# Loads, weights and a new hand-written order in a fused linear-attention and MLP kernel

## The chip, the cores and the metric

The kernel runs on one core of one Trainium2 chip. The metric is the device time of one execution in microseconds (us), lower is better; the profile's span runs from the first to the last instruction of the same program.

## The reference

Two pre-norm blocks in a row on 2048 tokens of width 512, all in bf16. Layer norm here has no weights. Block A is linear attention with 32 heads of 16 columns, block B a two-layer perceptron with 1792 hidden columns.

```python
def _A_ref(x, wqkv, wo):                       # H = 32, Dh = 16
    qkv = (lambda x, *d: x.transpose(*d))((x @ wqkv).reshape(B, S, 3, H, Dh), 2, 0, 3, 1, 4)
    q, k, v = qkv[0], qkv[1], qkv[2]
    phi = lambda t: jnp.where(t > 0, t + 1, jnp.exp(t)) + 1e-6
    pq, pk = phi(q), phi(k)
    kv = jnp.einsum("bhsd,bhse->bhde", pk, v)
    z = jnp.einsum("bhsd->bhd", pk)
    num = jnp.einsum("bhqd,bhde->bhqe", pq, kv)
    den = jnp.einsum("bhqd,bhd->bhq", pq, z)[..., None] + 1e-6
    o = num / den
    return (lambda x, *d: x.transpose(*d))(o, 0, 2, 1, 3).reshape(B, S, D) @ wo

h = x + _A_ref(_layernorm(x, axis=-1), A_wqkv, A_wo)
h2 = h + _B_ref(_layernorm(h, axis=-1), B_w1, B_w2)      # relu(ln(h) @ w1) @ w2
```

## The kernel before

The 2048 tokens are 16 tiles of 128 rows (t = 0 to 15) in 4 chunks of 512 (c = 0 to 3); the 512 columns are 4 blocks of 128, the 1792 hidden columns 14. There is no loop over tiles in the code. A string, ORDER (lines 18 to 55), lists 568 words; each word is the name of a small function with its numbers (`K.7.3` is `op_K(7, 3)`), and the last lines walk the string and issue the instructions. So the order of the words of one engine is the order in which that engine executes; words of different engines stand in for each other only through the semaphores that the data need. The last number of a word on TensorE is mostly the PSUM bank (of 8) that it writes.

The words by engine, in the order of the stages:

- **SP**, the only engine that issues DMAs, all of them into one queue: `lx.t.n` loads n tiles of x from tile t; `lk`, `lq`, `lv`, `lo`, `l1`, `l2` load the weights for keys, queries, values, output, w1 and w2 (first block of 128 rows, number of blocks); `X.t` and `x.t` are transposing DMAs (lines 290 and 291) that write one tile of the normed x, or of the normed h, transposed into lnT; `wb.c` (line 450) writes the reciprocal denominators of chunk c to DRAM, eight `rb.c.h` (line 453) read them back, broadcast, into one buffer rr; `fd.t` stores a tile of the result. The weights l2 come in two halves of 7 blocks, `l2.0.7` and `l2.7.7`.
- **TensorE**: `warm` (matmuls of zeros at the start), `T` and `t` (transposes of a tile), `K.t` (keys of one tile, line 298, 4 matmuls of 512 columns), `Q.c.j` (queries, line 306), `G.t` (the state of keys against the normed x, line 350, into banks 4 to 7), `z`, `d4.c` (denominators of a chunk, line 422), `kv`, `m` (m = kv times wo), `h.t` (attention output, line 475), `p.c.f` and `ph` (first layer, line 490 and in halves 499), `f.t.b.f0.n` (second layer, line 519, 14 matmuls in two halves of 7).
- **ScalarE (ACT)**: `R` and `r` (reciprocal standard deviation, two steps), `E` (a transposed tile from PSUM to lnT), `F` and `U` (exp and relu of the keys), `qF` and `qU` (of the queries), `dl4` and `dx4` (logarithm and exp that make the reciprocal denominators), `gA`, `mA` (copies of G and m), `pA` (relu of the first layer), `nA` (the centred h, line 257).
- **VectorE (DVE)**: `S` and `A`, `s` and `a` (mean and variance), `N` and `n` (normed x, centred h), `M` and `D`, `qM` and `qD` (min and sum that finish the feature maps), `za` to `zh` (sum of the keys), `gD`, `mD` (copies), `kx`, `dm.c.jb.2` (line 466: queries times rr into pqs), `hD` (line 481: h), `pD` (relu of the first layer, line 510), `fo` (result).

Around the change the chain of one chunk is: `d4.c` on TensorE, `dl4.c` and `dx4.c` on ScalarE, `wb.c` and eight `rb.c` on SP, two `dm.c` on VectorE, then four `h` on TensorE, of which each reads all four blocks of pqs. rr has one buffer, so `rb` of a chunk waits for `dm` of the chunk before. pqs has eight blocks, two chunks. All loads of weights are free of waits for data. The words of SP before, from the start to the second chunk's `rb`:

```
lx.0.1 lx.1.1 lx.2.2 lk.0.2 lk.2.2 lx.4.2 lx.6.2 lq.0.4 lx.8.4 lx.12.4 X.5 X.6 X.7 lv.2.2 lv.0.2
X.8 X.9 X.13 X.12 X.11 X.10 X.14 X.15 lo.0.2 lo.2.2 l1.0.2 l1.2.2 wb.0 rb.0 (8) l2.0.7 wb.1 x.1 x.0 rb.1 (8) l2.7.7
```

Of the kernel before, what the change touches and what calls it, by code (L numbers as in the profile page):

```python
# [15 lines left out]


ORDER = """
table const masks warm.70.7.64 warm.2.7 lx.0.1 S.0 lx.1.1 S.1 A.0 R.0.1 A.1 lx.2.2 S.2 N.0.0.2 A.2 N.0.2.2 R.1.1
R.2.1 N.1 T.0.4.0.2 E.0.0.2 T.0.3.2.2 lk.0.2 S.3 lk.2.2 T.1.7 lx.4.2 N.2 A.3 E.0.2.2 E.1 lx.6.2 R.3.1 lq.0.4 S.4  # L20
N.3 K.0.0.0.2 K.0.0.2.2 T.2.5 E.2 S.5 A.4 K.1.6.0.2 S.6 F.0.1 K.1.6.2.2 T.3.1 E.3 K.2.3.0.2 K.2.3.2.2 U.1.1 A.5
lx.8.4 R.4.2 S.7 M.0.1 U.0.1 A.7 A.6 N.4 R.6.2 N.5 D.0.1 S.9 K.3.2.0.2 K.3.2.2.2 Q.0.3.1 F.1.1 T.4.0 F.3.1 M.1.1
Q.0.1.5 N.6 M.3.1 A.9 N.7 D.1.1 E.4 Q.0.0.4 lx.12.4 K.4.6 F.2.1 M.2.1 U.2.1 U.3.1 S.13 D.3.1 X.5 S.8 qF.0.0.2
A.13 K.5.7 Q.0.2.0 X.6 K.6.2 qU.0.0.2 F.4.2 U.4.2 S.11 X.7 lv.2.2 A.8 S.12 D.2.1 A.12 M.4.2 S.10 R.8.2 R.12.2
lv.0.2 K.7.3 qM.0.0.2 G.2 U.6.2 G.3 G.1 G.0 N.8 A.11 A.10 N.9 X.8 X.9 N.13 D.4.2 S.14 S.15 R.10.2 F.6.2 A.14
qU.0.2.2 X.13 N.12 A.15 N.11 qD.0.0.2 M.6.2 N.10 G.4 X.12 R.14.2 K.8.2 G.5 qF.0.2.2 D.6.2 qM.0.2.2 N.14 za.4.1
N.15 K.9.3 F.8.2 G.7 K.13.1 U.8.2 K.12.0 M.8.2 X.11 za.6.0 X.10 G.6 U.12.2 X.14 K.11.3 X.15 D.8.2 F.12.2
qD.0.2.2 K.10.2 F.10.2 U.10.2 K.14.0 za.8.0 M.12.2 zf M.10.2 lo.0.2 K.15.1 F.14.2 G.9 G.8 U.14.2 zhi D.10.2
D.12.2 M.14.2 zlo G.10 Q.1.1.3 D.14.2 z.2.1 lo.2.2 l1.0.2 z.0.1 z.1.1 z.3.1 zc G.14 zh d4.0.0 G.11 G.13 G.12
dl4.0 G.15 gD.0.2 Q.1.0.2 dx4.0 Q.1.2.0 l1.2.2 gA.2.2 kv.2.7 kv.0.7 kv.1.7 kv.3.7 qF.1.0.2 qU.1.0.2 qM.1.0.2  # L30
Q.1.3.1 Q.2.1.5 kx qD.1.0.2 m.0.2 m.3.7 m.2.6 m.1.3 qF.1.2.2 qU.1.2.2 qM.1.2.2 mD.2.2 Q.2.0.4 wb.0 Q.2.2.0
rb.0.0 Q.2.3.1 mA.0.2 rb.0.1 rb.0.6 rb.0.7 rb.0.4 rb.0.2 rb.0.3 rb.0.5 qF.2.0.2 dm.0.0.2 dm.0.2.2 h.1.2 qU.2.0.2
qD.1.2.2 hD.1 d4.1.5 s.1 a.1 qU.2.2.2 h.0.4 hD.0 l2.0.7 h.3.7 n.1 dl4.1 dx4.1 s.0 qF.2.2.2 a.0 n.0 h.2.2 hD.2
wb.1 hD.3 Q.3.1.5 Q.3.0.4 s.2 x.1 Q.3.2.6 x.0 s.3 Q.3.3.7 a.2 rb.1.2 rb.1.1 a.3 n.2 qF.3.0.2 qU.3.0.2 n.3
ph.0.0.2.0 t.2.5 t.3.4 qM.2.0.2 rb.1.0 rb.1.5 rb.1.7 rb.1.6 qM.2.2.2 r.0.4 qF.3.2.2 ph.0.2.0.0 ph.0.1.3.0 v.2
v.3 qM.3.0.2 ph.0.3.1.0 ph.0.1.3.1 qM.3.2.2 qD.2.2.2 rb.1.3 rb.1.4 qD.2.0.2 qU.3.2.2 l2.7.7 ph.0.0.2.1 qD.3.0.2
qD.3.2.2 ph.0.2.0.1 pA.0.0.2 ph.0.3.1.1 p.0.10.6 d4.2.2.2 dm.1.0.2 dm.1.2.2 dl4.2 dl4.3 dx4.2 wb.2 pD.0.2.2
dx4.3 rb.2.0 p.0.11.7 pD.0.10.2 h.4.2 hD.4 h.6.3 h.7.5 hD.6 rb.2.6 hD.7 s.4 h.5.6 rb.2.3 p.0.6.0 rb.2.2 s.6 a.4
hD.5 s.7 a.6 s.5 p.0.7.1 a.7 n.4 p.0.5.7 p.0.4.6 pA.0.6.2 rb.2.5 rb.2.7 rb.2.1 a.5 p.0.12.5 n.7 pD.0.4.2 n.6
p.0.9.4 rb.2.4 p.0.8.3 wb.3 x.7 x.4 n.5 dm.2.2.2 x.6 dm.2.0.2 p.0.13.6 f.0.1.0.7 h.9.2 pD.0.8.2 pD.0.12.2 hD.9  # L40
r.4.4 h.8.3 h.11.0 s.9 hD.8 h.10.2 x.5 rb.3.4 rb.3.3 rb.3.2 rb.3.7 rb.3.6 hD.11 p.1.1.5 hD.10 a.9 p.1.0.4 s.8
p.1.9.3 s.10 s.11 rb.3.1 p.1.8.2 a.10 a.8 a.11 pA.1.0.2 n.8 rb.3.0 r.8.4 n.10 n.9 f.0.1.7.7 f.1.7.0.7 pA.1.8.2
rb.3.5 dm.3.2.2 n.11 dm.3.0.2 fo.0 h.15.6 hD.15 x.11 h.14.5 s.15 hD.14 h.12.3 p.1.12.0 h.13.4 a.15 p.1.13.1
hD.12 s.14 s.12 hD.13 a.12 pA.1.12.2 f.1.7.7.7 a.14 s.13 a.13 r.12.4 n.13 fo.1 n.12 n.15 n.14 p.1.5.2 p.1.4.1
pD.1.4.2 x.9 x.10 x.8 p.1.2.5 p.1.3.6 pD.1.2.2 p.1.10.0 p.1.11.1 p.1.6.5 x.13 p.1.7.6 pA.1.10.2 pA.1.6.2 p.2.4.2
p.2.5.3 f.3.7.0.7 f.2.5.0.7 f.3.7.7.7 f.2.5.7.7 pA.2.4.2 x.15 fo.3 p.2.12.2 p.2.13.3 p.2.1.1 p.2.0.0 pA.2.12.2
pA.2.0.2 p.2.8.3 p.2.9.4 p.2.6.1 p.2.7.2 fo.2 fd.3 pD.2.6.2 pA.2.8.2 p.2.3.4 p.2.2.3 f.4.5.0.7 x.14 fd.2 fd.0
x.12 pA.2.2.2 f.4.5.7.7 fo.4 f.5.0.0.7 f.5.0.7.7 fd.1 p.3.2.5 p.3.3.6 fo.5 f.7.7.0.7 f.6.1.0.7 f.6.1.7.7 fo.6
p.3.7.3 p.3.6.2 f.7.7.7.7 fo.7 pA.3.2.2 pA.3.6.2 p.3.0.6 p.3.10.4 p.3.1.7 pA.3.0.2 p.3.11.5 p.3.9.3 pD.3.10.2
p.3.4.0 p.3.5.1 pA.3.4.2 p.3.8.2 fd.7 p.3.12.6 p.3.13.7 pD.3.8.2 p.2.11.3 pD.3.12.2 f.15.0.0.14.0.2 p.2.10.2  # L50
f.8.5.0.7 fo.15.0.2 pD.2.10.2 f.8.5.7.7 fd.5 f.13.4.0.7 fd.6 fd.4 f.13.4.7.7 fo.8 fd.8 fd.15.0.2 f.9.3.0.7 fo.13
fd.13 f.9.3.7.7 f.14.0.0.7 fo.9 f.14.0.7.7 fo.14 f.11.7.0.7 f.11.7.7.7 fo.11 f.10.6.0.7 fd.14 f.10.6.7.7 fo.10
fd.9 fd.10 f.12.2.0.7 f.12.2.7.7 fo.12 fd.11 fd.12 f.15.0.0.14.3.1 fo.15.3.1 fd.15.3.1 f.15.1.0.14.2.1 fo.15.2.1
fd.15.2.1
"""


# [512 lines left out]
```

## Time and profile before

| what | value |
|---|---|
| time, median of 3 runs | 170.36 us (169.75 to 170.53) |
| the profiled execution | 169.94 us, its span 168.2 us |
| K, Q, G or h of one tile, four matmuls of 512 columns | 0.863 us from start to start of the next |
| eviction of 128x1024 from PSUM | ACT 1.02 us (L505), DVE 1.22 us (L510) |
| wb.0: issue, landing | 39.56 us, 41.27 us |
| rb.0: first issue, last landing | 41.28 us, 47.06 us |
| w1 halves: issue, landing | 30.53 and 31.04 us, 38.05 and 40.81 us |
| packets of 1 KB and of 3.5 KB on a DMA engine | 46 ns, 140 ns |

In the lines of the profile PE is TensorE's matmuls, PEld its weight loads, SPq the queue of SP. A line of the chain of waits has a start, a length and the work or the wait; a line of the list of waits has who waited for whom, the sum in us, how often, and the longest; a line of the timeline has a start, a length, the engine, the source line, and output and input. A DMA lands when all sixteen DMA engines have reported their part; a matmul's end in the trace is modelled, so the pace is read from starts.

### The profile page before, as it was taken

What the parts mean: (1) busy time and instruction counts of PE and PEld (TensorE: products, weight loads), DVE (VectorE), ACT (ScalarE), POOL (GpSimd) and SP (SyncE); (2) the same over time, 40 slices, a digit from 0 to 9 for tenths busy, and PEclk for the clock granted to TensorE, in tenths of its full rate; (3) what the DMA queues carried; (4) which work ended last, traced back from release to release, by engine and by line L of the source; (5) the groups of instructions that cost most, each with busy time, mean ns of one, the idle gap of its engine ahead of it and who ended that gap; (6) DMA issues with size and microseconds to landing.
All of it is one profiled execution on the core that took longest, in us unless ns stands there. A gap on an engine that the chain in (4) does not pass through costs nothing.

```text
span 168.2 us, 2427 instructions
## 1 busy us (share of the span) xinstructions
PE 163.7 (97%) x924; PEld 79.6 (47%) x924; DVE 99.1 (59%) x205; ACT 63.4 (38%) x97; POOL 4.7 (3%) x21
## 2 busy tenths in 40 slices
...
DMA packets 24875, 16.01 MB, mean 95 GB/s; under 512 B 15008, under 2 KB 23712, under 8 KB 24864
## 3 DMA queue, kind: packets, MB, share of 16 engines
...
q8 instruction: 7, 0.11, 0.3%
q14 instruction: 4, 0.03, 0.1%
...
## 4 chain that ended last, share of the span: by engine, by line
PE 91%; DVE 4%; DMA 2%; ACT 1%; issue 0%
PE bk L519 29%; PE bk L490 27%; PE bk L475 8%; PE bk L350 8%; PE bk L306 6%; PE bk L298 5%; PE bk L227 3%; PE bk L499 2%; DMA lnT<-h_nat 2%; DVE st L230 2%; PE bk L269 1%; DVE h_nat L244 1%; PE bk L422 1%; PE bk L374 1%; PE bk L396 1%; DVE eb L323 1%
## 5 line engine op out<-in xcount | busy, mean ns | idle before, releaser
L519 PE MATMUL bk<-w_sb,at 128*128 128x512 bf16 (+2 forms) x252 | 49.9, 355 | 0.0
L490 PE MATMUL bk<-lnT,w_sb 128*128 128x512 bf16 x208 | 46.9, 379 | 0.0
L505 ACT ACTIVATE at<-bk 128x1024 bf16<-128x1024 f32 x16 | 16.4, 1023 | 56.1 <-PE bk L490 39.4
L527 DVE SCALAR_TENSOR_TENSOR gT<-bk,rstd,h_nat 128x512 bf16<-128x512 f32 (+2 forms) x18 | 12.4, 691 | 40.1 <-PE bk L519 40.0
L519 PEld LDWEIGHTS <-at 128*128 128x128 bf16 x252 | 23.6, 98 | 25.4
L490 PEld LDWEIGHTS <-w_sb 128*128 128x128 bf16 x208 | 20.2, 98 | 24.4 <-issue 0.7
L510 DVE TENSOR_SCALAR at<-bk 128x1024 bf16<-128x1024 f32 x12 | 14.5, 1220 | 12.7 <-PE bk L490 12.7
L316 ACT ACTIVATE eb<-bk 128x1024 bf16<-128x1024 f32 (+1 forms) x18 | 16.7, 932 | 5.6 <-PE bk L298 2.8
L319 ACT ACTIVATE rb<-bk 128x1024 bf16<-128x1024 f32 (+1 forms) x18 | 16.7, 943 | 0.7 <-PE bk L298 0.7
L298 PE MATMUL bk<-wk_sb,lnT 128*128 128x512 bf16 x64 | 15.5, 379 | 0.6 <-DMA lnT<-h_nat 0.6
L306 PE MATMUL bk<-lnT,wq_sb 128*128 128x512 bf16 x64 | 15.1, 379 | 0.0
L475 PE MATMUL bk<-m_sb,pqs 128*128 128x512 bf16 x64 | 14.8, 379 | 0.0
L350 PE MATMUL bk<-at,h_nat 128*128 128x512 bf16 x56 | 13.4, 379 | 0.0
L230 DVE BATCH_NORM_STATS2 st<-x_nat 128x6 f32<-128x512 bf16 x16 | 10.6, 676 | 1.9 <-DMA x_nat<-in_A_x_dram 1.9
L481 DVE TENSOR_TENSOR h_nat<-bk,x_nat 128x512 bf16<-128x512 f32 x16 | 10.5, 678 | 1.4 <-PE bk L475 1.4
L232 DVE BATCH_NORM_STATS2 st<-h_nat 128x6 f32<-128x512 bf16 x16 | 10.4, 678 | 0.1
L475 PEld LDWEIGHTS <-pqs 128*128 128x128 bf16 x64 | 6.1, 98 | 7.7 <-DVE pqs L466 0.4
L298 PEld LDWEIGHTS <-lnT 128*128 128x128 bf16 x64 | 6.0, 98 | 7.8 <-DMA lnT<-h_nat 1.1
L350 PEld LDWEIGHTS <-h_nat 128*128 128x128 bf16 x64 | 6.1, 98 | 7.3 <-issue 0.2
L306 PEld LDWEIGHTS <-wq_sb 128*128 128x128 bf16 x64 | 6.2, 98 | 7.1
L323 DVE TENSOR_SCALAR eb<-eb 128x1024 bf16<-128x1024 bf16 (+1 forms) x18 | 6.8, 389 | 2.5 <-ACT eb L316 2.5
L244 DVE TENSOR_SCALAR h_nat<-x_nat,mv,rstd 128x512 bf16<-128x512 bf16 (+1 forms) x17 | 6.4, 393 | 0.1
...
## 6 DMA issues: line engine op xcount, KB each, us to landing
...
```

The lines of the kernel that those rows point to most:

```text
L230: op_S = lambda t: nc.vector.bn_stats(out=st[:, t, :], in_=x_nat[:, t, :])
L298: nc.tensor.matmul(bk[:, b, :], lhsT=lnT[c][:, kd, j * P : (j + 1) * P], rhs=wk_sb[:, kd, :], start=(kd == 0), stop=(kd == KD - 1),)
L306: nc.tensor.matmul(bk[:, b, :], lhsT=wq_sb[:, kd, j * P : (j + 1) * P], rhs=lnT[c][:, kd, :], start=(kd == 0), stop=(kd == KD - 1),)
L316: nc.scalar.activation(out=buf(eb, kind, i, n), in_=bank(at_bank[kind, i], n), func=ACT.Exp)
L319: nc.scalar.activation(out=buf(rb, kind, i, n), in_=bank(at_bank[kind, i], n), func=ACT.Relu)
L350: nc.tensor.matmul(bk[:, KD + kd, :], lhsT=ln_nat[:, t, kd * P : (kd + 1) * P], rhs=pk(t)[:, 0, :], start=(not stated), stop=(len(stated) ...
L475: nc.tensor.matmul(bk[:, b, :], lhsT=pqs[:, (c * KD + jb) % NQ, j * P : (j + 1) * P], rhs=m_sb[:, jb, :], start=(jb == 0), stop=(jb == KD ...
L490: nc.tensor.matmul(bk[:, b, :], lhsT=w1_sb[:, kd, f * P : (f + 1) * P], rhs=lnT[c][:, kd, :], start=(kd == 0), stop=(kd == KD - 1),)
L505: nc.scalar.activation(out=acts[c % 2][:, f : f + n, :], in_=bank(at_bank["p", c, f], n), func=ACT.Relu, scale=-1.0)
L510: nc.vector.tensor_scalar(out=acts[c % 2][:, f : f + n, :], in0=bank(at_bank["p", c, f], n), scalar1=-1.0, scalar2=0.0, op0=ALU.mult, op1= ...
L519: nc.tensor.matmul(bk[:, b, 0 : w * P], lhsT=acts[c % 2][:, f, j * P : (j + 1) * P], rhs=w2_sb[:, f, k * P : (k + w) * P], start=(f == 0), ...
L527: nc.vector.scalar_tensor_tensor(out=o_t[:, t % NO, cols], in0=bk[:, at_bank["f", t, k], 0 : w * P], scalar=rstd2[:, t : t + 1], in1=h_nat ...
```

## The change

Only the string ORDER changes; no function does. The diff replaces its 36 lines as a whole; the lines that hold the words spoken of are these (words of the same engine keep their order from line to line):

```diff
-table const masks warm.70.7.64 warm.2.7 lx.0.1 S.0 lx.1.1 S.1 A.0 R.0.1 A.1 lx.2.2 S.2 N.0.0.2 A.2 N.0.2.2 R.1.1
-R.2.1 N.1 T.0.4.0.2 E.0.0.2 T.0.3.2.2 lk.0.2 S.3 lk.2.2 T.1.7 lx.4.2 N.2 A.3 E.0.2.2 E.1 lx.6.2 R.3.1 lq.0.4 S.4
...
-A.13 K.5.7 Q.0.2.0 X.6 K.6.2 qU.0.0.2 F.4.2 U.4.2 S.11 X.7 lv.2.2 A.8 S.12 D.2.1 A.12 M.4.2 S.10 R.8.2 R.12.2
-lv.0.2 K.7.3 qM.0.0.2 G.2 U.6.2 G.3 G.1 G.0 N.8 A.11 A.10 N.9 X.8 X.9 N.13 D.4.2 S.14 S.15 R.10.2 F.6.2 A.14
...
-Q.1.3.1 Q.2.1.5 kx qD.1.0.2 m.0.2 m.3.7 m.2.6 m.1.3 qF.1.2.2 qU.1.2.2 qM.1.2.2 mD.2.2 Q.2.0.4 wb.0 Q.2.2.0
-rb.0.0 Q.2.3.1 mA.0.2 rb.0.1 rb.0.6 rb.0.7 rb.0.4 rb.0.2 rb.0.3 rb.0.5 qF.2.0.2 dm.0.0.2 dm.0.2.2 h.1.2 qU.2.0.2
-qD.1.2.2 hD.1 d4.1.5 s.1 a.1 qU.2.2.2 h.0.4 hD.0 l2.0.7 h.3.7 n.1 dl4.1 dx4.1 s.0 qF.2.2.2 a.0 n.0 h.2.2 hD.2
...
+table const masks warm.70.7.64 warm.2.7 lx.0.1 S.0 lx.1.1 S.1 A.0 R.0.1 lx.2.1 A.1 R.1.1 lk.0.2 S.2 N.0.0.2 A.2
+N.0.2.2 T.0.3.0.2 R.2.1 T.0.5.2.2 lx.3.1 lk.2.2 N.1 T.1.7 E.0.0.2 E.0.2.2 lx.4.2 K.0.4.0.2 S.3 A.3 K.0.4.2.2 N.2
...
+S.12 S.8 U.4.2 F.4.2 M.2.1 A.8 S.14 A.12 X.6 X.7 Q.0.3.1 S.13 K.6.2 K.7.3 U.3.1 R.8.2 D.2.1 A.14 A.13 S.10 S.11
...
+M.14.2 zlo G.7 G.11 lv.2.2 U.14.2 D.14.2 z.3.1 z.1.1 z.2.1 z.0.1 lv.0.2 lo.0.2 qF.1.0.2 qU.1.0.2 qM.1.0.2 lo.2.2
+G.8 l1.0.2 zc zh d4.0.2 G.12 G.15 l1.2.2 dl4.0 dx4.0 G.10 G.14 G.13 qD.1.0.2 Q.1.3.1 Q.1.2.0 gA.0.2 gD.2.2
+kv.3.2 kv.2.2 l2.0.7 kv.0.2 kv.1.2 Q.2.0.4 Q.2.1.5 kx qF.1.2.2 qM.1.2.2 wb.0 rb.0.5 rb.0.3 m.0.2 m.1.3 qU.1.2.2
+m.2.6 mA.0.2 m.3.7 Q.2.3.1 rb.0.2 Q.2.2.0 rb.0.4 mA.2.2 qD.1.2.2 qF.2.0.2 rb.0.1 rb.0.7 rb.0.6 rb.0.0 dm.0.0.2
+dm.0.2.2 h.1.2 hD.1 s.1 h.0.3 qU.2.2.2 hD.0 qF.2.2.2 a.1 h.3.7 h.2.6 s.0 hD.2 a.0 n.0 d4.1.1 Q.3.0.2 Q.3.1.3
+l2.7.7 hD.3 s.2 nA.1 s.3 Q.3.3.7 x.1 a.2 qU.2.0.2 dl4.1 dx4.1 a.3 qF.3.0.2 qU.3.0.2 Q.3.2.6 n.2 n.3 t.2.4
...
```

What it does, by parts:

- `lx.2.2` becomes `lx.2.1` and `lx.3.1`, with `lk.0.2` between them and `lk.2.2` behind: SP has one DMA more (98).
- `lv.2.2` and `lv.0.2` go from behind X.7 to behind X.15; `l2.0.7` from behind the `rb.0` to ahead of `wb.0`; `l2.7.7` from behind the `rb.1` to behind the `rb.0`. The eight `rb.3` go ahead of `x.4` to `x.7`.
- `mD.2.2` becomes `mA.2.2`, `n.1` becomes `nA.1`; of the 28 evictions of the first layer ACT has 17 instead of 16, DVE 11 instead of 12.
- Within each engine the words stand in another order, and many have another PSUM bank. Among them: on TensorE `d4.1` behind the four `h` of chunk 0 instead of behind the first; five instead of four `G` behind `d4.0`; the second half of `f.0` and the first of `f.3` ahead of chunk 1's first `p`. The number of matmuls of each kind stays.

The words of SP after, to the second chunk's `rb`:

```
lx.0.1 lx.1.1 lx.2.1 lk.0.2 lx.3.1 lk.2.2 lx.4.2 lx.6.2 lq.0.4 lx.8.4 lx.12.4 X.5 X.6 X.7
X.8 X.9 X.13 X.12 X.11 X.10 X.14 X.15 lv.2.2 lv.0.2 lo.0.2 lo.2.2 l1.0.2 l1.2.2 l2.0.7 wb.0 rb.0 (8) l2.7.7 x.1 x.0 wb.1 rb.1 (8)
```

More of the change, by code (lines that the diff above doesn't have):

```diff
@@ L18 @@
 ORDER = """
-table const masks warm.70.7.64 warm.2.7 lx.0.1 S.0 lx.1.1 S.1 A.0 R.0.1 A.1 lx.2.2 S.2 N.0.0.2 A.2 N.0.2.2 R.1.1
-R.2.1 N.1 T.0.4.0.2 E.0.0.2 T.0.3.2.2 lk.0.2 S.3 lk.2.2 T.1.7 lx.4.2 N.2 A.3 E.0.2.2 E.1 lx.6.2 R.3.1 lq.0.4 S.4
-N.3 K.0.0.0.2 K.0.0.2.2 T.2.5 E.2 S.5 A.4 K.1.6.0.2 S.6 F.0.1 K.1.6.2.2 T.3.1 E.3 K.2.3.0.2 K.2.3.2.2 U.1.1 A.5
-lx.8.4 R.4.2 S.7 M.0.1 U.0.1 A.7 A.6 N.4 R.6.2 N.5 D.0.1 S.9 K.3.2.0.2 K.3.2.2.2 Q.0.3.1 F.1.1 T.4.0 F.3.1 M.1.1
-Q.0.1.5 N.6 M.3.1 A.9 N.7 D.1.1 E.4 Q.0.0.4 lx.12.4 K.4.6 F.2.1 M.2.1 U.2.1 U.3.1 S.13 D.3.1 X.5 S.8 qF.0.0.2
@@ L24 @@
-A.13 K.5.7 Q.0.2.0 X.6 K.6.2 qU.0.0.2 F.4.2 U.4.2 S.11 X.7 lv.2.2 A.8 S.12 D.2.1 A.12 M.4.2 S.10 R.8.2 R.12.2
-lv.0.2 K.7.3 qM.0.0.2 G.2 U.6.2 G.3 G.1 G.0 N.8 A.11 A.10 N.9 X.8 X.9 N.13 D.4.2 S.14 S.15 R.10.2 F.6.2 A.14
-qU.0.2.2 X.13 N.12 A.15 N.11 qD.0.0.2 M.6.2 N.10 G.4 X.12 R.14.2 K.8.2 G.5 qF.0.2.2 D.6.2 qM.0.2.2 N.14 za.4.1
-N.15 K.9.3 F.8.2 G.7 K.13.1 U.8.2 K.12.0 M.8.2 X.11 za.6.0 X.10 G.6 U.12.2 X.14 K.11.3 X.15 D.8.2 F.12.2
-qD.0.2.2 K.10.2 F.10.2 U.10.2 K.14.0 za.8.0 M.12.2 zf M.10.2 lo.0.2 K.15.1 F.14.2 G.9 G.8 U.14.2 zhi D.10.2
@@ L29 @@
-D.12.2 M.14.2 zlo G.10 Q.1.1.3 D.14.2 z.2.1 lo.2.2 l1.0.2 z.0.1 z.1.1 z.3.1 zc G.14 zh d4.0.0 G.11 G.13 G.12
-dl4.0 G.15 gD.0.2 Q.1.0.2 dx4.0 Q.1.2.0 l1.2.2 gA.2.2 kv.2.7 kv.0.7 kv.1.7 kv.3.7 qF.1.0.2 qU.1.0.2 qM.1.0.2
-Q.1.3.1 Q.2.1.5 kx qD.1.0.2 m.0.2 m.3.7 m.2.6 m.1.3 qF.1.2.2 qU.1.2.2 qM.1.2.2 mD.2.2 Q.2.0.4 wb.0 Q.2.2.0
-rb.0.0 Q.2.3.1 mA.0.2 rb.0.1 rb.0.6 rb.0.7 rb.0.4 rb.0.2 rb.0.3 rb.0.5 qF.2.0.2 dm.0.0.2 dm.0.2.2 h.1.2 qU.2.0.2
-qD.1.2.2 hD.1 d4.1.5 s.1 a.1 qU.2.2.2 h.0.4 hD.0 l2.0.7 h.3.7 n.1 dl4.1 dx4.1 s.0 qF.2.2.2 a.0 n.0 h.2.2 hD.2
@@ L34 @@
[L34 to L53, printed above, removed]
@@ L54 @@
-fd.15.2.1
+table const masks warm.70.7.64 warm.2.7 lx.0.1 S.0 lx.1.1 S.1 A.0 R.0.1 lx.2.1 A.1 R.1.1 lk.0.2 S.2 N.0.0.2 A.2
+N.0.2.2 T.0.3.0.2 R.2.1 T.0.5.2.2 lx.3.1 lk.2.2 N.1 T.1.7 E.0.0.2 E.0.2.2 lx.4.2 K.0.4.0.2 S.3 A.3 K.0.4.2.2 N.2
+T.2.6 S.4 E.1 lx.6.2 R.3.1 E.2 N.3 lq.0.4 K.1.0.0.2 K.1.0.2.2 T.3.3 U.0.1 S.5 E.3 K.2.1.0.2 A.4 A.5 R.4.2
+K.2.1.2.2 K.3.7.0.2 S.6 S.7 lx.8.4 N.4 F.0.1 Q.0.0.2 T.4.6 M.0.1 A.6 A.7 N.5 K.3.7.2.2 Q.0.1.3 U.1.1 F.2.1 F.1.1
+S.9 D.0.1 R.6.2 M.1.1 Q.0.2.0 E.4 K.4.5 N.6 F.3.1 lx.12.4 N.7 D.1.1 A.9 X.5 U.2.1 M.3.1 qU.0.0.2 K.5.6 qF.0.0.2
@@ new lines @@
+S.12 S.8 U.4.2 F.4.2 M.2.1 A.8 S.14 A.12 X.6 X.7 Q.0.3.1 S.13 K.6.2 K.7.3 U.3.1 R.8.2 D.2.1 A.14 A.13 S.10 S.11
+R.12.2 D.3.1 N.8 M.4.2 A.10 A.11 N.9 N.13 X.8 D.4.2 F.6.2 G.1 S.15 M.6.2 G.0 G.2 G.3 G.5 X.9 A.15 R.10.2
+qF.0.2.2 N.10 N.12 U.6.2 N.11 qM.0.2.2 qM.0.0.2 D.6.2 qD.0.0.2 G.4 R.14.2 qU.0.2.2 X.13 K.8.2 N.14 K.9.3
+qD.0.2.2 za.4.1 F.8.2 X.12 G.6 K.13.1 K.12.0 U.8.2 M.8.2 X.11 K.11.3 F.12.2 N.15 D.8.2 X.10 U.12.2 K.10.2 F.10.2
+G.9 X.14 K.14.0 U.10.2 X.15 za.6.0 M.12.2 za.8.0 K.15.1 M.10.2 D.12.2 zf D.10.2 zhi F.14.2 Q.1.0.2 Q.1.1.3
@@ new lines @@
+l2.7.7 hD.3 s.2 nA.1 s.3 Q.3.3.7 x.1 a.2 qU.2.0.2 dl4.1 dx4.1 a.3 qF.3.0.2 qU.3.0.2 Q.3.2.6 n.2 n.3 t.2.4
+qM.3.0.2 qM.2.2.2 t.3.1 x.0 wb.1 rb.1.7 ph.0.2.0.0 r.0.4 rb.1.1 rb.1.5 ph.0.1.3.0 ph.0.0.2.0 qF.3.2.2 v.2 v.3
+ph.0.1.3.1 qU.3.2.2 qD.3.0.2 qM.2.0.2 qD.2.2.2 rb.1.2 rb.1.3 qM.3.2.2 ph.0.0.2.1 qD.2.0.2 ph.0.3.1.0 ph.0.2.0.1
+qD.3.2.2 ph.0.3.1.1 p.0.10.6 pA.0.0.2 d4.2.4.2 rb.1.4 rb.1.6 pD.0.2.2 rb.1.0 p.0.11.7 dl4.2 dx4.2 p.0.5.1 wb.2
+p.0.4.0 pD.0.10.2 p.0.9.4 dm.1.0.2 dm.1.2.2 pD.0.4.2 dl4.3 h.7.6 hD.7 h.4.3 hD.4 p.0.6.0 h.6.6 s.7 s.4 h.5.5 a.7
@@ new lines @@
+hD.6 p.0.8.3 a.4 rb.2.7 rb.2.6 rb.2.5 rb.2.4 rb.2.2 p.0.7.1 dx4.3 rb.2.0 hD.5 n.7 pA.0.6.2 rb.2.3 rb.2.1
+p.0.13.7 p.0.12.6 pD.0.8.2 pA.0.12.2 dm.2.0.2 dm.2.2.2 h.9.1 s.6 s.5 a.6 h.11.5 a.5 n.6 hD.9 n.5 s.9 hD.11 wb.3
+rb.3.1 rb.3.3 a.9 rb.3.7 n.4 s.11 n.9 rb.3.4 h.10.4 a.11 rb.3.2 f.0.6.0.7 rb.3.0 h.8.0 hD.10 f.0.6.7.7 rb.3.6
+rb.3.5 f.3.7.0.7 x.6 x.7 x.5 x.4 hD.8 dm.3.2.2 dm.3.0.2 s.10 s.8 h.14.5 a.10 a.8 r.4.4 h.15.2 n.11 n.8 hD.14
+n.10 hD.15 s.14 h.13.4 h.12.5 x.8 hD.13 a.14 s.15 x.10 s.13 r.8.4 p.1.12.1 hD.12 a.13 a.15 s.12 n.14 p.1.13.2
```

11 lines of the change are left out of this document (added).

## The prediction

> **What bounds the kernel now.** The page's shares first, then the chain of waits.
>
> ```profile
> PE 163.7 (97%) x924; PEld 79.6 (47%) x924; DVE 99.1 (59%) x205; ACT 63.4 (38%) x97; POOL 4.7 (3%) x21
> PE 91%; DVE 4%; DMA 2%; ACT 1%; issue 0%
> ```
>
> ```profile
> 14.15 3.44 DMA lnT<-h_nat
> 17.63 1.04 PE bk L298 x4
> ...
> 49.49 0.86 PE bk L475 x4
> ...
> 142.68 22.73 PE bk L519 x126
> 165.41 0.03 issue
> ```
>
> TensorE is the limit. From the K of tile 7 (17.63) to the last matmul (165.41) the chain never leaves it, and a matmul of 512 columns takes 0.216 us from start to start (K of four: 0.863). All that an order can win lies ahead of 17.63: 0.72 us of idle array before that K (matmul starts 16.69 and 17.63, less 0.216), and about 0.5 us until the first transposes (5.64, after the second wide warming matmul began at 5.19). An order can lose anywhere, if a product comes late. The list of waits and the timeline (engines, then SP's queue) show the two nearest to being late:
>
> ```profile
> DVE pqs L466 <- DMA rr<-scr: 1.1, 1, 1.1
> PE bk L298 <- DMA lnT<-h_nat: 0.6, 1, 0.6
> ```
>
> ```profile
> 46.72 1.22 DVE L414 CAST m_sb<-bk 128x1024 bf16<-128x1024 f32 x1
> 47.86 1.28 DVE L466 TENSOR_TENSOR pqs<-pqT,rr 128x1024 bf16<-128x1024 bf16 x2
> 49.33 1.03 PE L475 MATMUL bk<-m_sb,pqs 128*128 128x512 bf16 x4
> ```
>
> ```profile
> 29.40 1.08 SPq L216 DMA_DIRECT2D wo_sb<-in_A_wo_dram  x2
> 30.52 0.98 SPq L216 DMA_DIRECT2D w_sb<-in_B_w_dram  x2
> 39.56 0.34 SPq L450 DMA_DIRECT2D scr<-rd  x1
> 41.28 3.65 SPq L453 DMA_DIRECT2D rr<-scr  x8
> 44.97 0.43 SPq L216 DMA_DIRECT2D w_sb<-in_B_w_dram  x1
> ```
>
> The first h product (L475, 49.33) follows the scaling dm.0 (L466, two of 0.68 us started 0.60 apart) by 0.2 us, and dm.0 follows a DMA chain: wb.0 issued 39.56, landed 41.27; eight rb.0 issued from 41.28, the last landed 47.06, 5.80 after wb.0. Ahead of wb.0 in the queue stood the two halves of w1, issued at 30.5 and 31.0; the second landed at 40.81, 9.8 us after its issue. All DMAs of the kernel go through this one queue and start their packets in the order of issue. So wb.0 met a queue that had just run empty.
>
> **The change, part by part.**
>
> (a) *Tiles 2 and 3 apart.* One issue more on SP (0.41 to 0.42 us, rows of x tiles 0 and 1). The loads behind it already stand in a queue (time to landing grows from 2.15 to 8.17 us over the ten loads), so the issue costs nothing; if the queue were empty, 0.42. Tiles 2 and 3 landed together at 4.62; tile 2 alone, 128 KB behind tile 1 (3.30; tiles 0 and 1 landed 0.34 apart), comes at about 3.65 to 4.0. Then VectorE starts S.2 behind A.1 at 4.39 instead of 4.64, N.0 at 4.97 instead of 5.26 (just behind rstd at 4.91). Gain at the first transposes 0.25 to 0.29; I take 0.28. The weight wk and tile 3 (S.3 at about 5.9) arrive earlier than used.
>
> (b) *What follows.* Between E.1 and R.8 ScalarE has the same 18 steps in another order and is almost unbroken (R.8 at 17.90). So N.8, and with it the eight transposing DMAs X.8 to X.15 (start to start 1.31), also come 0.28 earlier, and X.15's issue ends at 29.07 instead of 29.35. X.7 goes out at about 13.9 instead of 14.15.
>
> (c) *wv behind X.15.* X.7 landed 3.44 after its issue, its neighbours 2.45; wv's first half was issued right behind X.7 (15.42). Freed of this, X.7 lands at 16.35, the K of tile 7 starts at 16.62, and TensorE is 1.0 early. Against it: X.15 with wo right behind took 2.42, and an 8 KB instruction fetch ran at 16.03, in the middle of X.7's packets. If the fetch is the cause, it stays and 0.28 is all. Bounds 0.28 to 1.0 early here.
>
> (d) *The weights' place.* Behind X.15 now stand wv (2 x 256 KB), wo (2 x 256 KB), w1 (2 x 896 KB), and now also the first half of w2 (896 KB), which used to follow rb.0; then wb.0. wb.0's issue needs dl4 and dx4 of d4.0 and comes 0.3 to 1.0 earlier, near 38.6 to 39.3, but its packets wait behind all this:
>
> w1's second half landed at 40.81; minus 0.28; wv adds 32 packets of 1 KB per DMA engine, 46 ns each: 1.47; w2's half 56 packets: 2.58; wb.0's own 8: 0.37. wb.0 lands at 40.81 - 0.28 + 1.47 + 2.58 + 0.37 = 44.95.
>
> From both sides: five of the sixteen engines finished w1 about 2 us behind the others (landings 37.97 to 38.78, and 39.95 to 40.81). If they share evenly, 42.9. If all 3.80 MB flow at the 345 GB/s of the window 34.5 to 38, from 30.2, 11.0 us, and wb.0 lands at 41.9. At the 236 GB/s that the 2.36 MB from 30.5 to 40.5 made, 16.1 us: about 47.0. I take 44.6, near the engine sum, a little less since the lag may not repeat in full.
>
> The Trainium skill, DMA: Bandwidth & Descriptors, section Specifications, puts the limit of HBM at about 358 GB/s for a core; the trace's 345 agrees. By the rule alone 3.80 MB would be over at 40.8 and wb.0 at 41.5, with no stall; the row of the whole stretch speaks against it.
>
> (e) *What is late next.* SP waits at rb.0 for wb.0, and w2's other half, x.1, x.0 and wb.1 queue behind; that half's 2.6 us of packets are through before x.1 is due. dm.0's second half ends 5.80 + 0.05 + 0.60 + 0.68 after wb.0, and the third matmul of h.1 (it reads that half) starts 0.05 later: 44.6 + 7.18 = 51.8, where it was 49.76. **Loss 2.0 us**, whatever (a) to (c) won: they end in front of this wait. Break-even is wb.0 at 42.6. Behind h.1 in TensorE's queue stands everything else, so the 2.0 goes to the end.
>
> (f) *Steps that change engine.* m's second copy from DVE (1.22) to ACT (1.03): DVE is free for dm.0 when rr lands, so the 0.80 between landing and dm.0 in the profile is gone (already in e). n.1 to ACT: x.1 is issued 2.95 instead of 2.66 after h.1's end, x.0 lands 6.7 after it, the first ph starts 6.8 after it (three h, d4, four Q, eight transposes): hidden by 0.1; a further 1 us late would cost 0.9. One of 28 evictions goes to ACT (1.02 for 1.22): hidden by the 56.1 us that ACT idles ahead of L505.
>
> (g) *d4.1 behind four h, rb.3 ahead of x.4 to x.7.* Counted from h.1's end: wb.1 is issued at 5.5, rb.1's last lands at 13.0, dm.1 is done at 15.4 (behind pD of blocks 10 and 11), the h that needs its second half is at 15.8. rb.2 may write rr only after dm.1: it lands at 21.2, dm.2 is done at 23.2 (behind pD of blocks 8 and 9), the third matmul of h.9 is at 23.5. The x of chunk 1 pass the eight rb.3 (8 x 0.46 = 3.7 us of SP), which wait for dm.2, and land by 33.3; the chunk's first p now stands behind two f halves and four h more, at 34.5. All covered, by 0.4, 0.3 and 1.2 us. The other reordered p, f and banks find each bank free at least 0.4 us before its next use, with evictions of 1.02 and 1.22 against two to four groups of 0.86 between. Zero, from 0 to +0.5.
>
> **Sum.** Own time 169.94 (span 168.23 and 1.71 around it) + 2.0 = 171.9. The median shown is 0.42 above it: 172.4.
>
> **Rivals.**
> *No block* (faster): wb.0 lands before 42.6, as at the 345 GB/s above. Then the front's gain stays: X.7 freed, 170.36 - 1.0 = 169.4; fetch to blame, 170.1. For it: 0.93 DMA share from 34.5 to 38. Against: nothing of that stretch held the rate from the first packet to the last. It decides below 42.6.
> *Half a block*: engines even, wb.0 at 42.9 to 43.4, loss 0.3 to 0.8: 170.9.
> *A colder array*: TensorE would stand idle from 48.3 to 49.0 on until 51.3, 2.3 to 3 us; before, its longest pause in the run was 0.72. In the first microseconds a wide matmul took 0.41 and full rate came only by 6.74, 5.7 us after the first matmul. If the pause brings that back, 4 to 5.7 us at half rate lose 2 to 2.8: about 174.8. A granted clock of 1.00 throughout speaks neither way. The Trainium skill, TensorE: Matmul & The Clock Gate, section What's actually happening, says that half rate follows an idle window of about 3.4 us; by that rule the pause is just too short, and the trace of before has none to test it.
>
> **Chances and range.** Forecast 0.60 (171.3 to 173.9); half a block 0.14; no block 0.19 (about half at 169.4); cold array 0.07. One in two hundred, 0.85 us, is what a measurement here can tell from none. Faster 0.13 (most of the no block case with X.7 freed, and some for what I have missed), within 0.18, slower 0.69. Range 169.7 to 173.9: it leaves out the colder array and the best of no block; the forecast's own range is 171.3 to 173.9.
>
> **What would show it.** Right: wb.0 issued near 39 and landing past 44; a TensorE gap of 2 to 3 us before the first L475, released by L466 behind rr<-scr; K of tile 7 earlier by 0.3 to 1.0 and that gain gone at h.1; no gap afterwards. Wrong: wb.0 landing within 2.5 us of its issue, or the first L475 before 49.3; or new gaps behind 60 us, which would make the step (g) wrong.

## The result, and the profile after

| kernel | time, median | ratio to before, 95% interval |
|---|---|---|
| before | 170.26 us (169.75 to 170.53, 4 runs) | |
| after | 172.82 us (172.2 to 174.31, 4 runs) | 1.0158 [1.0126, 1.0191] |

The change makes the kernel 1.6% slower. The profiled execution of after took 174.31 us, its span 172.6 (before 168.2), 1.5 above the median, and that has a reason of its own: two losses lie on top of each other. A run more than 1.5% above the fastest of its kernel is left out of every ratio here (two runs of the kernel with wv back, one of the repeat of after), so there the ratio is lower than the median alone gives. The page's busy shares and chain shares come first, then the chain of waits (start, length, what).

```profile
PE 165.3 (96%) x924; PEld 79.9 (46%) x924; DVE 95.8 (55%) x202; ACT 66.3 (38%) x100; POOL 4.7 (3%) x21
PE 84%; DMA 8%; SPq 4%; ACT 1%; issue 1%; DVE 1%; DVEq 0%
```

```profile
4.64 6.61 DMA wq_sb<-in_A_wqkv_dram
...
39.92 5.24 DMA scr<-rd
48.37 2.64 DMA rr<-scr
51.32 0.70 DVE pqs L466
52.07 5.49 PE bk L475 x16
...
145.46 24.26 PE bk L519 x140
```

Before, the chain stayed on TensorE from 17.63 to the end. Now its front goes through the queries' weight, which lands at 11.25 (before 9.65), and later it leaves TensorE for wb.0 (5.24 us from issue to landing, 1.71 before), the last rb.0 and dm.0, and comes back at 52.07, where the first h began at 49.33: 2.74 later. The same 924 matmuls are busy for 165.3 instead of 163.7 us, and the sixteen of chunk 0's h take 5.49, where full rate makes 3.45 of them (4 x 0.863). Most of that difference is the second loss. The list of waits and the timeline of SP's queue:

```profile
DVE pqs L466 <- DMA rr<-scr: 3.9, 1, 3.9
PE bk L475 <- DVE pqs L466: 2.2, 1, 2.2
PE bk L298 <- DMA wk_sb<-in_A_wqkv_dram: 0.8, 1, 0.8
```

```profile
30.50 1.09 SPq L216 DMA_DIRECT2D wv_sb<-in_A_wqkv_dram  x2
31.63 0.98 SPq L216 DMA_DIRECT2D wo_sb<-in_A_wo_dram  x2
32.65 1.49 SPq L216 DMA_DIRECT2D w_sb<-in_B_w_dram  x3
39.92 0.34 SPq L450 DMA_DIRECT2D scr<-rd  x1
45.17 3.62 SPq L453 DMA_DIRECT2D rr<-scr  x8
48.84 0.43 SPq L216 DMA_DIRECT2D w_sb<-in_B_w_dram  x1
```

Three loads of 896 KB now stand right ahead of wb.0. The second half of w1 landed at 42.52 (before 40.81), the first half of w2 at 44.86, wb.0 at 45.16, 0.30 behind it; SP stood at the first rb.0 from 40.3 to 45.17. The wait L298 <- wk_sb is new, and it is at the front: the second half of wk landed at 7.63, before at 6.13.

The second loss in a table by stretches: the length, the busy time of PE, PEld, DVE, ACT, POOL with instructions in brackets, then the granted TensorE clock (1.00 is full speed), the DMA share and GB/s.

```profile
48.00:52.00 4.00, 1.85 (x9) 0.65 (x7) 0.68 (x2) 4.00 (x5) 0.00 (x0) 1.00 0.64 178
52.00:53.40 1.40, 1.33 (x5) 0.42 (x6) 0.63 (x3) 0.42 (x1) 0.00 (x0) 0.94 0.98 345
53.40:56.80 3.40, 3.40 (x10) 1.27 (x9) 2.79 (x5) 1.03 (x2) 0.00 (x0) 0.52 0.03 8
56.80:60.00 3.20, 3.20 (x19) 1.25 (x18) 2.30 (x6) 2.17 (x4) 0.00 (x0) 1.00 0.20 41
```

From 53.4 to 56.8 the mean clock is 0.52, and the row counts only ten matmuls. Inside it their starts are 0.427 apart instead of 0.216: ten steps from 53.12 to 56.96 took 3.84 instead of 2.16, 1.7 us lost. 2.74 + 1.7 is the 4.4 by which the span grew.

### The profile page after: what moved, and what is told of

The parts are those of the page before. It is cut to its first block, busy times and chain, and to the rows that moved or that the text cites. A ratio compares the mean times of both kernels' runs of the same rounds, so it can differ in the third digit from the quotient of the medians.

```text
span 172.6 us, 2431 instructions
## 1 busy us (share of the span) xinstructions
PE 165.3 (96%) x924; PEld 79.9 (46%) x924; DVE 95.8 (55%) x202; ACT 66.3 (38%) x100; POOL 4.7 (3%) x21
## 4 chain that ended last, share of the span: by engine, by line
PE 84%; DMA 8%; SPq 4%; ACT 1%; issue 1%; DVE 1%; DVEq 0%
PE bk L519 28%; PE bk L490 26%; PE bk L475 9%; PE bk L298 6%; PE bk L350 6%; PE bk L306 5%; DMA wq_sb<-in_A_wqkv_dram 4%; DMA scr<-rd 3%; PE bk L499 2%; SPq L453 2%; DMA rr<-scr 2%; SPq L213 2%; PE bk L422 1%; PE bk L374 1%; SPq L216 1%
## 5 line engine op out<-in xcount | busy, mean ns | idle before, releaser
L505 ACT ACTIVATE at<-bk 128x1024 bf16<-128x1024 f32 x17 | 17.4, 1022 | 46.9 <-PE bk L490 31.9
L510 DVE TENSOR_SCALAR at<-bk 128x1024 bf16<-128x1024 f32 x11 | 13.4, 1223 | 17.8 <-PE bk L490 17.8
L475 PE MATMUL bk<-m_sb,pqs 128*128 128x512 bf16 x64 | 16.7, 411 | 2.2 <-DVE pqs L466 2.2
L298 PE MATMUL bk<-wk_sb,lnT 128*128 128x512 bf16 x64 | 15.5, 379 | 0.8 <-DMA wk_sb<-in_A_wqkv_dram 0.8
L475 PEld LDWEIGHTS <-pqs 128*128 128x128 bf16 x64 | 6.5, 105 | 11.5 <-DVE pqs L466 3.2
L298 PEld LDWEIGHTS <-lnT 128*128 128x128 bf16 x64 | 6.0, 98 | 7.7 <-issue 1.0
L236 ACT ACTIVATE rstd<-mv,eps 128x2 f32<-128x2 f32 (+2 forms) x14 | 4.1, 295 | 10.0 <-DVE mv L233 7.6
L466 DVE TENSOR_TENSOR pqs<-pqT,rr 128x1024 bf16<-128x1024 bf16 x8 | 5.1, 685 | 3.9 <-DMA rr<-scr 3.9
```

Of the source, the lines that this page charges most:

```text
L298: nc.tensor.matmul(bk[:, b, :], lhsT=lnT[c][:, kd, j * P : (j + 1) * P], rhs=wk_sb[:, kd, :], start=(kd == 0), stop=(kd == KD - 1),)
L475: nc.tensor.matmul(bk[:, b, :], lhsT=pqs[:, (c * KD + jb) % NQ, j * P : (j + 1) * P], rhs=m_sb[:, jb, :], start=(jb == 0), stop=(jb == KD ...
L505: nc.scalar.activation(out=acts[c % 2][:, f : f + n, :], in_=bank(at_bank["p", c, f], n), func=ACT.Relu, scale=-1.0)
L510: nc.vector.tensor_scalar(out=acts[c % 2][:, f : f + n, :], in0=bank(at_bank["p", c, f], n), scalar1=-1.0, scalar2=0.0, op0=ALU.mult, op1= ...
```

## The experiments

In all kernels but the repeat of after, two lines of the source fewer (a shorter ORDER) put L466 at L464 and L475 at L473. Each ran beside runs of the kernel before.

**The first half of w2, alone.** In the order of before only this word moves:

```diff
- ... l1.0.2 l1.2.2 wb.0 rb.0 (8) l2.0.7 ...
+ ... l1.0.2 l1.2.2 l2.0.7 wb.0 rb.0 (8) ...
```

> The kernel before with one word moved: the first half of w2 goes ahead of wb.0. Theory queue: wb.0 lands at 40.81 + 2.58 + 0.37 = 43.8 instead of 41.27, dm.0 ends 6.9 to 7.1 later, the third matmul of the first h starts near 51.0 instead of 49.76, and the time is 171.3 to 171.8 (+0.6 to +0.9%). Rival order: no step of an engine changes, so 170.3 (within 0.2%).

Measured: 171.41 us (171.31 to 172.5), ratio 1.0094 [1.0069, 1.012]. SP's queue in the timeline:

```profile
39.48 0.34 SPq L448 DMA_DIRECT2D scr<-rd  x1
43.79 3.62 SPq L451 DMA_DIRECT2D rr<-scr  x8
```

The half landed at 43.43, wb.0 at 43.77, 4.30 after its issue; the first h began at 50.62, 1.59 after the matmul before it. No run of it had a mean granted clock below 1.0. So one word costs 0.9% without anything else of the change.

**The same word taken back in the new order.**

```diff
- ... l1.2.2 l2.0.7 wb.0 rb.0 (8) l2.7.7 ...
+ ... l1.2.2 wb.0 rb.0 (8) l2.0.7 l2.7.7 ...
```

> The new order with one word moved: the first half of w2 goes back behind the eight rb.0. Theory queue (the weights that stand ahead of wb.0 in the one DMA queue cost the time): the 56 packets of 46 ns are gone from ahead of wb.0, it lands about 2.6 us sooner than 45.16, near 42.6, the first h starts at 49.5 to 50.0, and the time is 170.2 to 170.9 (0 to +0.4% against before). Rival order (the moved words of the engines cost it, whatever the queue): 172.2 to 172.9 as before this edit.

Measured: 170.12 (169.35 to 170.77), ratio 1.0005 [0.9979, 1.0031]. wb.0 was issued at 39.86 and landed at 42.33, and no gap stood ahead of the first h. With this word taken back, all that after loses is gone; everything else of the change together is worth nothing that this measurement can tell, with gains and losses inside it, as the next ones show.

**wv behind X.7 again, w2 as in after.**

```diff
- ... X.7 X.8 ... X.15 lv.2.2 lv.0.2 lo.0.2 ...
+ ... X.7 lv.2.2 lv.0.2 X.8 ... X.15 lo.0.2 ...
```

> The new order with wv's two loads back behind X.7, the half of w2 still ahead of wb.0. Theory queue: 32 packets of 46 ns less ahead of wb.0, it lands 1.5 us sooner than 45.16, near 43.7; the first h starts near 50.6; time 171.0 to 171.6 (+0.4 to +0.8%). Rival order: 172.2 to 172.9. On X.7: if a plain load right behind it delays its landing, 3.4 us from issue to landing; if the instruction fetch did that before, 2.4 to 2.5.

Measured: 172.18 (170.51 to 174.39), ratio 1.0094 [1.0057, 1.0131]; the four runs at full clock have a median of 171.76, a little above the forecast, so wv is worth less than was expected. wb.0 landed at 44.05, 13.96 behind the end of X.15's issue (30.09); in after 14.72 and 14.22 (the two profiles, 30.44 to 45.16 and 30.46 to 44.68). So wv's half megabyte has a share of 0.3 to 0.8 in the wait. Two of the six runs (173.64 and 174.39) had a mean granted clock of 0.99. And X.7, with wv right behind it, landed 2.44 after its issue, not 3.4: wv is not what delays X.7.

**Both taken back.**

```diff
- ... X.7 X.8 ... X.15 lv.2.2 lv.0.2 lo.0.2 lo.2.2 l1.0.2 l1.2.2 l2.0.7 wb.0 rb.0 (8) l2.7.7 ...
+ ... X.7 lv.2.2 lv.0.2 X.8 ... X.15 lo.0.2 lo.2.2 l1.0.2 l1.2.2 wb.0 rb.0 (8) l2.0.7 l2.7.7 ...
```

> The new order with wv behind X.7 and the half of w2 behind rb.0, so that only wo and w1 stand ahead of wb.0 as in the kernel before. Theory queue: wb.0 lands within 2 us of its issue or near 41.3, the first h starts when its banks and Q allow (49.0 to 49.7), and the time is 169.9 to 170.6 (-0.2 to +0.2%): the rest of the new order is worth nothing either way. Rival order: over 171.5.

Measured: 169.89 (169.71 to 170.75), ratio 1.0005 [0.998, 1.0029]. wb.0 landed at 42.21, the first h followed the matmul before it by 0.505 (0.505 less 0.216: 0.29 of it idle): this is about where the wait begins to decide. X.7 again took 2.46.

**Something for the array to do in the pause.** Ten matmuls of zeros, 512 columns each, whose result nobody reads, ahead of the first h of the new order:

```diff
- ... dm.0.2.2 h.1.2 ...
+ ... dm.0.2.2 warm.10.2 h.1.2 ...
```

> The new order with ten matmuls of 512 columns put ahead of the first h; they write the bank that the first h then overwrites, so they only keep the array busy for 2.16 us of its pause. Theory clock (about a quarter of the runs of the new order lose a further 1.7 us, since the pause of 2 to 2.4 us lets the array fall to half rate for 3.4 us): no run with a granted clock of 0.99, none above 173.2, the median 172.2 to 172.8. Rival (the slow runs have another cause, as loads that came late): the spread stays, with runs above 173.6, or the fillers themselves make it longer.

Measured: 173.1 (172.33 to 173.62), ratio 1.0151 [1.0118, 1.0184], and the clock 0.998 or above in all six runs. No run shows the half rate, but the time isn't better: in its profile the whole front was late (1.66 from start to start ahead of the transposes of tile 3 at 10.42, wb.0 issued at 41.10 and down at 46.07). VectorE shows where it began:

```profile
9.36 0.69 DVE L228 BATCH_NORM_STATS2 st<-x_nat 128x6 f32<-128x512 bf16 x1 [2.27 <-DMA x_nat<-in_A_x_dram]
```

In the new order the statistics of tile 4 stand ahead of the normed tile 3 on VectorE, and tiles 4 and 5 landed at 9.34 (in after 8.33). Why that load was late is open. The filler as a remedy is a miss. That the half rate belongs to the pause agrees with it, but six runs are few: with after's four in ten, six without it come by chance about once in twenty times (0.6 to the sixth, 0.047).

**The kernel after once more, to count the clock.** No edit.

> The changed kernel once more, to count the clock. If the pause of 2.4 ahead of the first h brings the half clock only in some executions, about a quarter to a third of the runs have a mean granted clock of 0.99 and take 173.6 or more, the others 172.0 to 173.2 at 0.998 or above. If the profiled execution was an accident of profiling alone, no timed run is at 0.99.

Measured: 173.27 (172.03 to 174.74, 6 runs), ratio 1.018 [1.0136, 1.0224]. Three runs at a clock of 0.988 to 0.990: 173.66, 174.18, 174.74; three at 0.998 or above: 172.03, 172.52, 172.88. More often than the quarter to third expected. This time the profiled execution was one of the others (span 170.3), with the same stretch:

```profile
53.40:56.80 3.40, 3.40 (x19) 1.39 (x18) 3.33 (x9) 1.86 (x3) 0.00 (x0) 1.00 0.00 0
```

Nineteen matmuls instead of ten. Its wb.0 landed at 44.68, its first h began at 51.50, 2.17 later than before, and the span is 2.1 longer than before's: without the half rate the wait is the whole loss. Over all ten runs of after, four at 0.99 have a mean of 174.2, six others 172.55: 1.7 apart, what the slow matmuls lose.

**The two single loads, alone.** In the order of before:

```diff
- lx.0.1 lx.1.1 lx.2.2 lk.0.2 lk.2.2 lx.4.2 ...
+ lx.0.1 lx.1.1 lx.2.1 lk.0.2 lx.3.1 lk.2.2 lx.4.2 ...
```

> The kernel before with nothing but tiles 2 and 3 as single loads around the first half of the keys' weight. Theory split: the second half of the keys' weight lands 1.0 to 1.8 later than 6.1 and the first K's second half waits for it by 0.3 to 1.0; the time rises to 170.4 to 171.0 (+0.2 to +0.5%). Theory as predicted on record (the loads arrive earlier than used): VectorE and the first transposes start 0.25 earlier, time 169.8 to 170.1.

Measured: 170.73 (170.35 to 171.98, 12 runs), ratio 1.0035 [1.0012, 1.0059]. A small loss, not a gain. TensorE's timeline:

```profile
7.52 0.59 PE L296 MATMUL bk<-wk_sb,lnT 128*128 128x512 bf16 x2 [0.58 <-DMA wk_sb<-in_A_wqkv_dram]
...
9.51 0.40 PE L267 MATMUL bk<-ident,h_nat 128*128 128x128 bf16 x4 [0.31 <-DVE h_nat L242]
```

Here TensorE waits 0.58 for the second half of wk, and then 0.31 for a normed tile. That half landed at 7.48 instead of 6.13, tiles 4 and 5 at 8.42 instead of 7.10, and X.7 was issued at 15.11 instead of 14.15.

**The new order without its slow parts: both weights back, tiles 2 and 3 in one load.** Run on two chips, the second time beside the same order with two loads.

```diff
- lx.0.1 lx.1.1 lx.2.1 lk.0.2 lx.3.1 lk.2.2 lx.4.2 ...
+ lx.0.1 lx.1.1 lx.2.2 lk.0.2 lk.2.2 lx.4.2 ...
```

> The kernel of the fourth run (wv and the half of w2 back) with tiles 2 and 3 in one load again, ahead of both halves of the keys' weight. Theory split (the single loads let some DMA engines fall behind, so that the second half of the keys' weight lands at 7.0 to 7.9 instead of 6.1 and tile 4 at 7.9 to 8.6 instead of 7.0): it lands near 6.1 and tile 4 near 7.1, the pauses of 0.4 to 1.2 us before the second half of the first K and of 0.2 to 0.4 before the fourth transpose are gone, X.7 still lands 2.45 after its issue, and the first G starts at 17.6 to 18.0. wb.0 is still held by w1, so the time gains less than the front: 169.2 to 169.8. Rival chance (the late landings come and go): the same pauses, 169.7 to 170.3.

> The new order with both moves of weights taken back and tiles 2 and 3 in one load, once more beside the same order with two single loads. If the single loads cost what they did in the old order (0.35%), this one is 0.3 to 0.6 us faster than its neighbour, at 169.5 to 169.9, ratio to before 0.995 to 0.999, with the second half of wk down before 6.5. Rival, the first interval (0.9939 to 1.0) was luck: 170.2, ratio 1.000.

> The same order with tiles 2 and 3 as two loads. By the late second half of wk (past 7.0) 170.0 to 170.4, 0.3 to 0.6 above its neighbour. Rival, the front has slack: both at the same time within 0.2.

Measured: 169.67 (168.88 to 171.17, 12 runs), ratio 0.9969 [0.9939, 1.0]; again 169.44 (168.86 to 170.94, 12 runs), ratio 0.995 [0.9914, 0.9987]. With two loads 169.99 (169.53 to 170.7, 12 runs), ratio 0.9974 [0.9946, 1.0002]. So 0.55 between the neighbours (0.52 in the order of before), and the one-load version is the fastest of the study, 0.3 and 0.5% ahead of before; the first of the two intervals reaches 1.0. Its profile, of the second run, SP's queue and then TensorE:

```profile
30.66 0.98 SPq L214 DMA_DIRECT2D w_sb<-in_B_w_dram  x2
38.93 0.34 SPq L448 DMA_DIRECT2D scr<-rd  x1
40.66 3.62 SPq L451 DMA_DIRECT2D rr<-scr  x8
44.32 1.03 SPq L214 DMA_DIRECT2D w_sb<-in_B_w_dram  x2
```

```profile
16.16 1.89 PE L296 MATMUL bk<-wk_sb,lnT 128*128 128x512 bf16 x8
17.88 1.89 PE L348 MATMUL bk<-pk_lo,h_nat 128*128 128x512 bf16 x8
...
48.70 3.62 PE L473 MATMUL bk<-m_sb,pqs 128*128 128x512 bf16 x16
```

wb.0 is down 1.71 after its issue, the keys of tiles 6 and 7 follow each other without the gap that before has at 17.63, the first G starts at 17.88 (before 18.51), and h runs at once. Its span is 167.4, 0.8 below before's.

**Other places for the halves.** On top of the one-load version, the second half of w1 behind rb.0, and the second half of w2 behind rb.1; then that half behind rb.2 instead:

```diff
- ... l1.0.2 l1.2.2 wb.0 rb.0 (8) l2.0.7 l2.7.7 x.1 x.0 wb.1 rb.1 (8) wb.2 rb.2 (8) wb.3 ...
+ ... l1.0.2 wb.0 rb.0 (8) l1.2.2 l2.0.7 x.1 x.0 wb.1 rb.1 (8) l2.7.7 wb.2 rb.2 (8) wb.3 ...
```

> The same as the run before it, with the second half of w1 also behind the eight rb.0 and the second half of w2 behind the eight rb.1. Theory queue: with a half of w1 the only 896 KB ahead of it, wb.0 lands 1.7 us after its issue, rr 5.8 later, and the first h starts as soon as its Q is done, 48.6 to 49.0; with the front of the run before, 168.8 to 169.5 (-0.4 to -0.8% against before). Rival: w1's second half comes too late for the first ph, whose start moves behind 57 us: 170 or more.

> The new order with tiles 2 and 3 in one load, wv behind X.7, the second half of w1 and the first of w2 behind rb.0 as in the run before, and the second half of w2 now behind the last rb.2. Queue theory (a small write behind a load of 896 KB is late; nothing else is wrong with this order): wb.0, wb.1 and wb.2 each land within 2.0 us of their issue, the pause of 2.01 ahead of the products of tile 9 is gone, and the time is 168.8 to 169.6, ratio 0.991 to 0.997. Rival, the half of w2 is now too late or holds wb.3: a pause of 0.5 to 2 ahead of the second half of f.0 near 80 us, or ahead of h.14, released by DMA w_sb or by rb.3; 170.2 to 171.5. Second rival, the pause in the previous run had other causes than the write: it stays, 170.8.

Measured: 170.8 (170.3 to 171.77), ratio 1.0035 [1.0014, 1.0056], and 172.36 (171.36 to 173.58), ratio 1.0144 [1.0099, 1.019]. Both lose against the version that they start from, against forecasts of 168.8 to 169.5 and 168.8 to 169.6, and each shows why in SP's queue:

```profile
60.74 0.43 SPq L214 DMA_DIRECT2D w_sb<-in_B_w_dram  x1
62.64 0.34 SPq L448 DMA_DIRECT2D scr<-rd  x1
```

```profile
70.10 0.40 SPq L214 DMA_DIRECT2D w_sb<-in_B_w_dram  x1
70.62 0.49 SPq L448 DMA_DIRECT2D scr<-rd  x1
76.95 1.25 SPq L451 DMA_DIRECT2D rr<-scr  x3
```

In the first wb.2 landed 3.73 after its issue, and tile 9's h at 74.39 started 2.01 behind the matmul ahead of it. In the second wb.2 took 1.71, as the queue theory had it, but wb.3 now stands half a microsecond behind the load and took 6.18: chunk 3's first h at 84.19 started 2.64 behind the matmul ahead of it. Two of the six runs had a clock of 0.99, the profiled one not. Part of the loss in this profile is a late front (first h at 49.60, in the one-load version 48.70). The forecast of a gain fell here, and the rival (the half holds wb.3) is what happened: I had not looked at what is issued next behind the last rb.2. The mechanism is the same at three places of the run: wb.0, wb.2 and wb.3.

## Why the prediction came out

The mechanism was right. That the size was right too is in part luck: two steps ahead of the wait were wrong and nearly cancelled, and the half rate, which four of ten runs had, was not in the forecast time.

**(d), the weights' place: right in sum, by luck.** Forecast landing of wb.0: 44.95 by the engine sum, 44.6 taken; measured 45.16 and 44.68 in two profiles. By terms, in the first: X.15's issue ended at 30.44 instead of 29.35, so the term -0.28 was +1.09; from there to w1's landing it was 12.08 instead of 11.46, so wv cost 0.62 and not 1.47; w2's half 2.34 for 2.58, wb.0 0.30 for 0.37. The lag of some DMA engines at w1 stayed (first and last landing 40.38 and 42.52). The errors are +1.37, -0.85, -0.24 and -0.07, together +0.21. wv's 0.62 agrees with the 0.3 to 0.8 of the kernel that has wv back; 1.47 was too much, and why was not tested. wb.0's issue came at 39.92 and 40.07, not near 38.6 to 39.3; that cost nothing, since its packets wait for the loads.

**(e), what is late next: right, but for 0.3.** The third matmul of h.1 was to start 7.18 behind wb.0's landing; it started 7.52 and 7.42 behind it. The term that was too small is the 0.05 between rb.0's last landing and dm.0: it took 0.32 in both profiles (51.00 to 51.32, and 50.43 to 50.75). The loss of 2.0 was 2.1 in the span of the execution without the half rate, and the six such runs have a mean of 172.55 for the 172.4 forecast (2.4 and 2.7 above the before that ran beside them). Break-even was put at 42.6; with wb.0 at 42.21 TensorE idled 0.29, at 42.33 in another profile not at all, since there the matmuls ahead of the first h ended 0.7 later: right within some tenths. That the front's gain or loss ends ahead of this wait also held: the late front of after costs it nothing visible, while in the order of before it costs 0.35%.

**(a), the single loads: the step that failed.** That wk and tile 3 arrive earlier than used is not so. The first transposes did come earlier in after (5.53 for 5.64), but the second half of wk landed at 7.03 to 7.93 in all eight profiles with two loads, and at 6.09 to 6.52 in five of six with one (7.94 in the sixth, where X.15's issue ended at 30.37, as late as in after). In after the first half of tile 0's keys begins at 6.28, so the second half of wk would be used at about 6.7; the keys wait for it until 7.67, and with tiles 4 and 5 also late the whole chain to X.15 shifts. In the trace the first engine to report is as early as before (5.82 in both), the last one isn't. Why some engines lag with two loads was not found out.

**(b), X.8 to X.15 0.28 earlier: wrong** with (a): 1.09 later in after. The K of tile 7, which was to start 0.3 to 1.0 earlier than 17.63, started at 18.00 and 18.37 in the two profiles of after.

**(c), wv and X.7: the second of the two causes named.** X.7 took 3.38 to 3.50 in the three profiles of the old order and 2.44 to 2.46 in all eleven of the new one, with wv behind it or not. In the trace's records of instruction fetches the 8 KB one comes 1.8 to 1.9 after X.7's issue in the old order, in the middle of its packets, and 2.6 to 3.5 after it in the new, when X.7 is down. That fits the fetch as the cause; the fetch alone was not moved, so it isn't shown by itself. The gap at 17.63 is gone, and in the one-load version, whose X.7 is issued at 14.46, the K of tile 7 starts at 17.02, 0.61 earlier than before. That its span is 0.8 shorter fits a gain that reaches the end; X.7 alone was not tried.

**(f), (g): right.** Behind 58 us after's profile has no idle time of TensorE over 0.05 us.

**The rivals.** *No block* rested on the rate of 345 GB/s. That rate came in after, for the greater part of the loads; the row has the same columns as the table above:

```profile
34.50:42.50 8.00, 8.00 (x76) 3.96 (x75) 2.55 (x6) 3.47 (x5) 0.00 (x0) 1.00 1.00 355
```

What the rival left out are the ends: from 30.5 to 32.5 the queue moved 123 GB/s, and from 43.0 to 45.2, when eleven of the sixteen DMA engines were done with wb.0 by 43.86 and the last five by 45.16, 91. The 3.80 MB from 30.5 to 45.16 made 259. The Trainium skill, DMA: Bandwidth & Descriptors, section Specifications, gives about 358 GB/s as the limit of HBM for a core; the trace agrees over those 8 us, and stands above it for a part (381 from 38.8 to 43.1), where the measurement decides. *Half a block* asked for even engines and wb.0 at 42.9 to 43.4; the engines stayed uneven. *A colder array* had 0.07, and about 174.8; it came in four of ten runs of after, at 174.2. Sized rightly but for 0.6, it was held too unlikely: the step that failed is that the pause would be too short. The Trainium skill, TensorE: Matmul & The Clock Gate, section What's actually happening, speaks of an idle window of about 3.4 us, free-running. The half rate did last 3.41 in the clock records, which is the length that the Trainium skill gives for that window, but the array had been empty for 2.4 only (the last matmul ahead of the pause began at 49.47 and takes 0.216, the next at 52.07). So the trace disagrees with the part on a whole idle window, and the measurement decides.
